# Splitting the third head group four and four, not six and two, between the two column halves of the tensor array

## The chip, the cores and the metric

One core of a Trainium2 chip runs the whole program. The metric is the time of one execution in microseconds (us); the time of a kernel is the median of its runs. "The profiled execution" is one run that was recorded by the hardware profiler: it has a time of its own, and a span, which reaches from its first to its last instruction.

Engines are named as the profile names them: PE is the tensor engine's matmul side, PEld its weight loads, DVE the vector engine, ACT the scalar engine, POOL the GpSimd engine, SP the engine whose queue issues the DMA transfers.

## The reference

Three stages follow each other: a recurrence over 768 steps for 32 heads (4 batches of 8) with a 40x40 state each, an attention layer with routed experts, and a token and channel mixer. The change is in the recurrence alone:

```python
for t in range(S):
    y[:, :, t] = np.einsum('bhd,bhde->bhe', rt, state)
    Sa = np.einsum('bhde,bhe->bhd', state, at)
    state_decay = state * wt[:, :, None, :] - np.einsum('bhd,bhe->bhde', Sa, bt)
    state = state_decay + np.einsum('bhd,bhe->bhde', vt, kt)
```

What comes after it is `_moe_ref` on y and `_moe2_ref` on that. The change touches neither.

## The kernel before

**Chunks and pairs.** The 768 steps are cut into 12 chunks of 64 steps; two chunks (an even and an odd one) make a pair. Inside a chunk, the sequential dependence is a triangular system for each head, whose inverse is worked out on DVE once for a whole pair: `solve` starts with a transpose `tp` (L226), runs 31 steps of two DVE instructions (`pr`, L235, and `x`, L237), and ends with the transpose `xt` (L240). The solve of the next pair runs on DVE, step by step among other work, while the chunks of this pair run on PE. `xt` is needed by the first `xz` of the next even chunk.

**Heads and groups.** The heads are packed three to a group of 120 partitions, so there are 11 groups; the last one holds two heads. `QUADS` collects them into three head groups q = 0, 1, 2 with 4, 4 and 3 groups, that is 12, 12 and 8 heads. This document is about q = 2: groups 8, 9 and 10, heads 24 to 31.

**Sides.** Many matmuls of the recurrence have a stationary operand of only 64 columns (one chunk of 64 steps) or 32 (half a chunk). The array has 128 columns, so such a matmul uses one half of them: side 0 writes PSUM partitions 0 to 63, side 1 partitions 64 to 127. `sides(q, n)` yields who goes to which side: the first two groups of a head group to side 0, the rest to side 1, in turns as long as both have some. With q = 0 and 1 that is six heads and six. With q = 2 it is heads 24 to 29 on side 0 and heads 30 and 31 on side 1, in the order 24, 30, 25, 31, 26, 27, 28, 29. `spans(q)` says which columns of the result lie on which side, for the instructions that read them back: 240 and 240, for q = 2 240 and 80.

**Steps of a chunk that use sides**, for each q:

- `z1` (L276): the state `ST` through the matrix `a`, one matmul for each group, 120 columns (80 for the last), into a PSUM tile `zu`; and in it
- `tv` half 0 (L289): one matmul for each head, 64 columns of weights and 40 moving, added to `zu`; then ACT takes the first 32 rows to `zt` (L293), one instruction for each side;
- `xz` half 0 (L302): one matmul for each head with 32 columns of weights; ACT takes the result to `vu` (L306);
- `tv` half 1 and `xz` half 1: the same for the second 32 rows, again with weights of 32 columns;
- `hh` (L357) and `yy` (L400), for the chunk before: like `z1` and `tv` half 0, into a PSUM tile `y`; DVE multiplies it into `ptt` (L404), one instruction for each side.

Every such fp32 matmul shows up in the trace as two loads and two matmuls.

**What sets the order.** `EVEN` and `ODD` are strings that list the steps of a chunk in the order in which the code issues them (a letter for the step, a digit for q); `x3` to `x5` are `xz` half 1. The order that then stands on each engine is not this one: a scheduler behind the language moves instructions by its own cost estimates, so any edit may move work far from it. Each engine works through its own list in that order. SP's list holds all loads and stores.

Of the kernel before, what the change touches and what calls it, by code (L numbers as in the profile page):

```python
# [28 lines left out]
G = 11  # L29
# [6 lines left out]
ODD = "A z0 x0 v0 v1 z1 z2 r0 h0 x2 t0 m1 x1 m2 s0 v2 r1 y0 h1 m0 r2 M y1 p0 L p1 p2 h2 y2 x3 t1 t2 d0 s2 k0 x5 s1 k1 x4 d2 k2 d1"  # L36
QUADS = [(0, 4), (4, 8), (8, 11)]

def sides(q, n):

    g0, g1 = QUADS[q]
    a, b, e = n * g0, n * (g0 + 2), min(n * g1, 32 if n > 1 else G)
    for i in range(b - a):
        yield a + i, 0, i
        if b + i < e:
            yield b + i, 1, i

def spans(q):

    g0, g1 = QUADS[q]  # L50
    return (0, 120 * g0, 240), (64, 120 * g0 + 240, min(120 * g1, 1280) - 120 * g0 - 240)

def nheads(g):
    return 2 if g == G - 1 else 3
# [15 lines left out]
class Rec:  # L70
# [199 lines left out]
    def z1(s, c, q):  # L270
        nc, t = s.nc, s.T[c // 2]
        zu = s.pz.tile([128, 480], F32, name="zu")
        s.T["zu", q] = zu
        for g, b, i in sides(q, 1):
            k = 40 * nheads(g)
            nc.tensor.matmul(zu[64 * b:64 * b + 64, 120 * i:120 * i + k], t["a"][:k, g, c % 2, :],  # L276
                             s.ST[:k, g, :k], start=(i == 0), stop=False, skip_group_check=True)
        s.tv(c, q, 0)

    def tv(s, c, q, half):  # L280

        nc = s.nc
        zu, sc, vu = s.T["zu", q], s.T["sc", c], s.T["vu", c]
        u = 64 * (1 - c % 2)
        r = slice(u, u + 64) if half else slice(0, 128)
        m = 32 if half else 64
        for h, b, i in sides(q, 3):
            o = 64 * b + 32 * half
            nc.tensor.matmul(zu[o:o + m, 40 * i:40 * i + 40], sc[r, h, 32 * half:32 * half + m],  # L289
                             vu[r, 40 * h:40 * h + 40], start=False, stop=True, skip_group_check=True)  # L290
        d = u + 32 * half
        for b, o, n in spans(q):
            nc.scalar.activation(s.zt[half][d:d + 32, o:o + n], zu[b + 32 * half:b + 32 * half + 32, :n], AF.Copy,  # L293
                                 scale=-1.0)

    def xz(s, c, q, half):
        nc = s.nc
        zu, xt, vu = s.T["zu", q], s.T["xt", c // 2], s.T["vu", c]
        r = slice(64 * (1 - c % 2), 64 * (1 - c % 2) + 64)
        for h, b, i in sides(q, 3):  # L300
            o = 64 * b + 32 * half
            nc.tensor.matmul(zu[o:o + 32, 240 + 40 * i:280 + 40 * i], xt[r, h, :],  # L302
                             s.zt[half][r, 40 * h:40 * h + 40], start=True, stop=True, skip_group_check=True)
        d = 64 * (1 - c % 2) + 32 * half
        for b, o, n in spans(q):
            nc.scalar.activation(vu[d:d + 32, o:o + n], zu[b + 32 * half:b + 32 * half + 32, 240:240 + n], AF.Copy)  # L306
# [44 lines left out]
    def hh(s, c, q):  # L351
        nc = s.nc
        y = s.ps.tile([128, 240], F32, name="y", bufs=1)
        s.T["y", q] = y
        for g, b, i in sides(q, 1):
            k = 40 * nheads(g)
            nc.tensor.matmul(y[64 * b:64 * b + 64, 120 * i:120 * i + k], s.T["r", c][:k, g], s.S[:k, g, :k],  # L357
                             start=(i == 0), stop=False, skip_group_check=True)

    def vut(s, c, q):  # L360
        nc, vu = s.nc, s.T["vu", c]
# [32 lines left out]
    def yy(s, c, q):  # L394
        nc = s.nc
        g0 = QUADS[q][0]
        d = 64 * (c % 2)
        y, sr, kbt = s.T["y", q], s.T["sr", q], s.T["kbt", c]
        for h, b, i in sides(q, 3):
            nc.tensor.matmul(y[64 * b:64 * b + 64, 40 * i:40 * i + 40], sr[:, h - 3 * g0, :], kbt[:, 40 * h:40 * h + 40],  # L400
                             start=False, stop=True, skip_group_check=True)
        xo = s.T["ptt", c // 2]
        for b, o, n in spans(q):
            nc.vector.tensor_tensor(xo[d:d + 64, o:o + n], y[b:b + 64, :n], xo[d:d + 64, o:o + n], OP.mult)  # L404
        if (c % 2, q) == (1, 2):
            nc.sync.dma_start(s.xd[64 * (c - 1):64 * (c + 1)], xo)
# [610 lines left out]
def channel(ctx, tc, ident, psum, ud, c1, c2, out, nb=4):  # L1017
# [19 lines left out]
    def first(s, m):  # L1037
        uh, ul, ur = X[s]
        ms = slice(128 * m, 128 * m + 128)
        p = psum()  # L1040
        mm = [(c1h[:, 0, ms], uh[:, 0]), (c1l[:, 0, ms], uh[:, 0]), (c1h[:, 1, ms], uh[:, 1]),
              (c1l[:, 1, ms], uh[:, 1]), (c1h[:, 2, ms], ur), (c1l[:, 2, ms], ur),
              (c1h[:, 0, ms], ul[:, 0]), (c1h[:, 1, ms], ul[:, 1])]
        for n, (l, r) in enumerate(mm):
            nc.tensor.matmul(p, l, r, start=(n == 0), stop=(n == 7))  # L1045
        hh = wk.tile([128, 512], F32R, name="hh", bufs=LAG + 2)
        hl = wk.tile([128, 512], F32R, name="hl", bufs=LAG + 2)
        nc.scalar.activation(hh, p, AF.Relu)  # L1048
        nc.vector.scalar_tensor_tensor(hl, p, 0.0, hh, op0=OP.max, op1=OP.subtract)  # L1049
        H[s, m] = hh, hl  # L1050
# [101 lines left out]
```

## Time and profile before

| | |
|---|---|
| time, median of 3 runs | 1045.84 us (1043.87 to 1049.55) |
| the profiled execution: its time | 1045.46 us |
| the profiled execution: its span | 1043.7 us |
| mean granted clock of TensorE over the span | 0.969 of full speed |
| busy: PE, PEld, DVE, ACT, POOL | 959.1, 823.1, 674.4, 479.3, 167.7 us |
| matmuls of L289 and L302 in the whole run | 1536 each |
| the chain that ended last: PE, DVE, DMA, ACT | 66%, 19%, 6%, 4% |

The recurrence fills the first 446 us or so, then come the other two stages. A busy share is an average over stages with different limits, and a busy PE is not a PE at its peak: its matmuls are pipelined and overlap. A row that merges several instructions (x24) gives the start of the first and the time until the end of the last. "Granted clock" is the share of TensorE's full clock of 2.4 GHz that the chip granted in a stretch.

### The profile page before, as it was taken

What the parts mean: (1) busy time and instruction counts of PE and PEld (TensorE: products, weight loads), DVE (VectorE), ACT (ScalarE), POOL (GpSimd) and SP (SyncE); (2) the same over time, 40 slices, a digit from 0 to 9 for tenths busy, and PEclk for the clock granted to TensorE, in tenths of its full rate; (3) what the DMA queues carried; (4) which work ended last, traced back from release to release, by engine and by line L of the source; (5) the groups of instructions that cost most, each with busy time, mean ns of one, the idle gap of its engine ahead of it and who ended that gap; (6) DMA issues with size and microseconds to landing.
All of it is one profiled execution on the core that took longest, in us unless ns stands there. A gap on an engine that the chain in (4) does not pass through costs nothing.

```text
span 1043.7 us, 23515 instructions
## 1 busy us (share of the span) xinstructions
PE 959.1 (92%) x9313; PEld 823.1 (79%) x9313; DVE 674.4 (65%) x1793; ACT 479.3 (46%) x1250; POOL 167.7 (16%) x214
## 2 busy tenths in 40 slices
PE   2977997999999999966999999999998999999998
PEld 1646876888888898855877888888787898898987
DVE  6598898887989685747898777566287222222222
ACT  1324544656665665534677667666543121121211
POOL 5000000010000000352234132223255000000000
PEclk9977996999999999979999999999999999999999
DMA  8604422417253323455543441420262101101000
GB/s 172 138 1 96 100 67 74 111 41 170 53 123 74 86 61 117 157 165 145 154 116 99 118 115 31 96 65 26 87 205 63 56 1 56 39 18 57 1 26 26
DMA packets 101031, 88.84 MB, mean 85 GB/s; under 512 B 60785, under 2 KB 91073, under 8 KB 100321
## 3 DMA queue, kind: packets, MB, share of 16 engines
q1 hardware_dynamic: 100921, 87.34, 32.2%
q8 instruction: 74, 1.21, 0.5%
q14 instruction: 36, 0.29, 0.1%
HBM read 54.94 MB, written 15.73 MB: 68 GB/s over the span
## 4 chain that ended last, share of the span: by engine, by line
PE 66%; DVE 19%; DMA 6%; ACT 4%; issue 3%; POOL 1%; SPq 1%; DVEq 0%; ACTq 0%; POOLq 0%
PE pq L1045 12%; PE p L1059 11%; PE psc L205 4%; PE zu L289 3%; PE psc L387 3%; DVE pq L164 3%; PE po L872 3%; PE pq L846 3%; PE zu L302 2%; PE pq L998 2%; PE pm L325 2%; PE zu L276 2%; DVE x L237 2%; PE y L400 2%; DVE pr L235 2%
## 5 line engine op out<-in xcount | busy, mean ns | idle before, releaser
L1049 DVE SCALAR_TENSOR_TENSOR hl<-pq,hh 128x512 fp32r<-128x512 f32 x72 | 49.7, 690 | 153.6 <-ACT hh L1048 153.6
L1048 ACT ACTIVATE hh<-pq 128x512 fp32r<-128x512 f32 x72 | 42.9, 596 | 186.7 <-PE pq L1045 186.7
L1059 PE MATMUL p<-c2h,hh 128*128 128x320 f32 x288 | 90.8, 315 | 0.0
L819 ACT ACTIVATE a<-s,nm 128x512 f32<-128x512 f32 (+3 forms) x128 | 68.7, 542 | 46.4 <-DVE nm L816 21.6
L1059 PE MATMUL p<-c2l,hh 128*128 128x320 f32 x288 | 89.4, 311 | 0.2 <-POOL c2l L635 0.2
L1059 PE MATMUL p<-c2h,hl 128*128 128x320 f32 x288 | 89.5, 311 | 0.1
L306 ACT ACTIVATE vu<-zu 32x240 f32<-32x240 f32 (+1 forms) x144 | 48.8, 339 | 55.2 <-PE zu L302 45.1
L293 ACT ACTIVATE zt<-zu 32x240 f32<-32x240 f32 (+1 forms) x144 | 48.7, 338 | 51.7 <-PE zu L289 49.6
L814 DVE TENSOR_REDUCE nm<-s 128x1 f32<-128x512 f32 (+3 forms) x128 | 62.0, 500 | 15.7 <-PE s L813 10.8
L164 DVE TENSOR_TENSOR pq<-w,pq 120x88 f32<-120x88 f32 x186 | 61.2, 329 | 9.7 <-DMA w<-in_w 5.8
L832 POOL TENSOR_TENSOR a<-a,rs 128x128 f32<-128x128 f32 (+1 forms) x64 | 45.6, 734 | 126.6 <-DVE rs L827 84.5
L235 DVE TENSOR_TENSOR pr<-tp,x 128x31 f32<-128x31 f32 (+15 forms) x186 | 63.0, 339 | 3.8 <-DVE tp L226 0.5
L237 DVE TENSOR_TENSOR x<-x,pr 128x31 f32<-128x31 f32 (+15 forms) x186 | 63.2, 340 | 3.3
L289 PE MATMUL zu<-vu,sc 64*32 64x40 f32 (+1 forms) x1536 | 61.3, 220 | 1.2 <-ACT vu L306 1.2
L302 PE MATMUL zu<-zt,xt 64*32 64x40 f32 x1536 | 48.3, 211 | 12.5 <-DVE pq L161 6.8
L1045 PE MATMUL pq<-uh,c1h 128*128 128x512 f32 x144 | 57.6, 400 | 0.8 <-DVE ul L666 0.8
L289 PEld LDWEIGHTS zu<-vu,sc 64*32 64x32 f32 (+1 forms) x1536 | 53.2, 127 | 6.2 <-ACT vu L306 2.9
L1059 PEld LDWEIGHTS p<-c2h,hh 128*128 128x128 f32 x288 | 54.5, 189 | 3.7 <-DVE o L1062 1.2
L1045 PE MATMUL pq<-uh,c1l 128*128 128x512 f32 x144 | 57.1, 396 | 0.0
L1059 PEld LDWEIGHTS p<-c2l,hh 128*128 128x128 f32 x288 | 54.5, 189 | 2.9 <-POOL c2l L635 0.5
L387 PE MATMUL psc<-rbd,vut 120*128 120x192 f32 (+1 forms) x264 | 54.6, 341 | 1.9 <-DVE sr L391 1.6
L302 PEld LDWEIGHTS zu<-zt,xt 64*32 64x32 f32 x1536 | 40.3, 117 | 20.1 <-issue 12.8
(206 smaller groups left out, 2504.4 us busy)
## 6 DMA issues: line engine op xcount, KB each, us to landing
kb<-in_kb SPq DMA_DIRECT2D x5, 1320.0 KB
kh<-hb SPq DMA_DIRECT2D x64, 96.0 KB
cv<-in_c SPq DMA_DIRECT2D x18, 256.0 KB
w<-in_w SPq DMA_DIRECT2D x6, 660.0 KB
a<-in_a SPq DMA_DIRECT2D x6, 660.0 KB
r<-in_r SPq DMA_DIRECT2D x12, 330.0 KB
rbd<-in_r SPq DMA_DIRECT2D x36, 110.0 KB
vu<-in_v SPq DMA_DIRECT2D x12, 320.0 KB
```

What stands on the lines that cost most here:

```text
L164: e.tensor_tensor(two(pq, i + 1, x + 29 - 2 * i), two(t["w"], i, 31 - 2 * i), two(pq, i, x + 31 - 2 * i), OP.mult)
L235: v.tensor_tensor(prv, tp[:, j + 1:, j:j + 1].to_broadcast([128, n, j + 1]), x[:, j:j + 1, :j + 1].to_broadcast([128, n, j + 1]), OP.mult)
L237: v.tensor_tensor(x[:, j + 1:, :j + 1], x[:, j + 1:, :j + 1], prv, OP.subtract)
L289: nc.tensor.matmul(zu[o:o + m, 40 * i:40 * i + 40], sc[r, h, 32 * half:32 * half + m], vu[r, 40 * h:40 * h + 40], start=False, stop=True, ...
L302: nc.tensor.matmul(zu[o:o + 32, 240 + 40 * i:280 + 40 * i], xt[r, h, :], s.zt[half][r, 40 * h:40 * h + 40], start=True, stop=True, skip_gr ...
L306: nc.scalar.activation(vu[d:d + 32, o:o + n], zu[b + 32 * half:b + 32 * half + 32, 240:240 + n], AF.Copy)
L387: nc.tensor.matmul(ps[:, n:n + nheads(g), :], vt[:k, g - g0, :], rbd[:k, g, :nheads(g), :], start=True, stop=True)
L814: nc.vector.tensor_reduce(nm[:, x:x + 1], s, axis=AX.X, op=OP.max, negate=True)
L819: nc.scalar.activation(a[:, n0:n1], s, AF.Exp, bias=nm[:, -1:] if nb_ == 2 else nm[:, :1], accum_out=sm[:, x, i % 2:i % 2 + 1])
L1045: nc.tensor.matmul(p, l, r, start=(n == 0), stop=(n == 7))
L1049: nc.vector.scalar_tensor_tensor(hl, p, 0.0, hh, op0=OP.max, op1=OP.subtract)
L1059: nc.tensor.matmul(Y[s][i], hs[x][:, ts], w[:, k], start=(k + n == 0), stop=(k == 11 and n == 2))
```

## The change

`sides` now counts heads, half to each side: for q = 2 heads 24 to 27 on side 0 and 28 to 31 on side 1, in turns. The border then runs through group 9, so `z1` and `hh`, which work by groups, need a new helper `blocks` that cuts a group where a side ends: group 8 (120 columns) and the first 40 columns of group 9 on side 0, the other 80 columns of group 9 and group 10 (80 columns) on side 1: four matmuls where three were. `spans` gives 160 and 160 columns for q = 2. For q = 0 and 1 the three functions yield what they did. Lines after them stand 13 lower.

```diff
-def sides(q, n):
+def blocks(q):
 
     g0, g1 = QUADS[q]
-    a, b, e = n * g0, n * (g0 + 2), min(n * g1, 32 if n > 1 else G)
-    for i in range(b - a):
-        yield a + i, 0, i
-        if b + i < e:
-            yield b + i, 1, i
+    m, e = 3 * g0 + (12 if g1 < G else 8) // 2, min(3 * g1, 32)
+    out = [[], []]
+    for z, (l, h) in enumerate(((3 * g0, m), (m, e))):
+        x = l
+        while x < h:
+            y = min(h, 3 * (x // 3) + 3)
+            out[z].append((x // 3, 40 * (x % 3), 40 * (x % 3 + y - x), z, 40 * (x - l)))
+            x = y
+    return [x for p in zip(*out) for x in p]
+
+def sides(q):
+
+    g0, g1 = QUADS[q]
+    n = (min(3 * g1, 32) - 3 * g0) // 2
+    for i in range(n):
+        yield 3 * g0 + i, 0, i
+        yield 3 * g0 + n + i, 1, i
 
 def spans(q):
 
     g0, g1 = QUADS[q]
-    return (0, 120 * g0, 240), (64, 120 * g0 + 240, min(120 * g1, 1280) - 120 * g0 - 240)
+    n = (min(120 * g1, 1280) - 120 * g0) // 2
+    return (0, 120 * g0, n), (64, 120 * g0 + n, n)
...
-        for g, b, i in sides(q, 1):
+        for g, l, h, b, o in blocks(q):
             k = 40 * nheads(g)
-            nc.tensor.matmul(zu[64 * b:64 * b + 64, 120 * i:120 * i + k], t["a"][:k, g, c % 2, :],
-                             s.ST[:k, g, :k], start=(i == 0), stop=False, skip_group_check=True)
+            nc.tensor.matmul(zu[64 * b:64 * b + 64, o:o + h - l], t["a"][:k, g, c % 2, :],
+                             s.ST[:k, g, l:h], start=(o == 0), stop=False, skip_group_check=True)
...
-        for h, b, i in sides(q, 3):
+        for h, b, i in sides(q):
...
-        for g, b, i in sides(q, 1):
+        for g, l, h, b, o in blocks(q):
             k = 40 * nheads(g)
-            nc.tensor.matmul(y[64 * b:64 * b + 64, 120 * i:120 * i + k], s.T["r", c][:k, g], s.S[:k, g, :k],
-                             start=(i == 0), stop=False, skip_group_check=True)
+            nc.tensor.matmul(y[64 * b:64 * b + 64, o:o + h - l], s.T["r", c][:k, g], s.S[:k, g, l:h],
+                             start=(o == 0), stop=False, skip_group_check=True)
```

On PE, in the fourth chunk, this is `z1` and `tv` half 0 for q = 1 and 2 before; the last three rows but one are `z1` of q = 2, the last is its `tv`, eight matmuls:

```order
L276 MATMUL zu<-ST,a 64x120 x4
L289 MATMUL zu<-vu,sc 64x40 x12
L276 MATMUL zu<-ST,a 64x120
L276 MATMUL zu<-ST,a 64x80
L276 MATMUL zu<-ST,a 64x120
L289 MATMUL zu<-vu,sc 64x40 x8
```

The same place now:

```order
L289 MATMUL zu<-ST,a 64x120 x4
L302 MATMUL zu<-vu,sc 64x40 x12
L289 MATMUL zu<-ST,a 64x120
L289 MATMUL zu<-ST,a 64x80
L289 MATMUL zu<-ST,a 64x40
L289 MATMUL zu<-ST,a 64x80
L302 MATMUL zu<-vu,sc 64x40 x8
```

`z1` of q = 2 has a matmul more and narrower ones; `tv` keeps its eight, whose sides an order does not show.

The scheduler also moved whole instructions. On DVE, around the `xt` of the fifth solve, which the ninth chunk waits for, before (`ptt` is `yy`'s result of the chunk before, `sc` and `sr` are masked products that DVE takes out of PSUM):

```order
L235 TENSOR_TENSOR pr<-tp,x 128x31
L237 TENSOR_TENSOR x<-x,pr 128x31
L240 STREAM_TRANSPOSE xt<-x 128x32x32
L404 TENSOR_TENSOR ptt<-y,ptt 64x240 x2
L210 TENSOR_TENSOR sc<-psc,mask 128x128
L391 TENSOR_TENSOR sr<-psc,mask 128x384 x3
L391 TENSOR_TENSOR sr<-psc,mask 128x128
L404 TENSOR_TENSOR ptt<-y,ptt 64x240 x2
```

The same place now:

```order
L404 TENSOR_TENSOR sr<-psc,mask 128x384
L248 TENSOR_TENSOR pr<-tp,x 128x60
L250 TENSOR_TENSOR x<-x,pr 128x2x30
L404 TENSOR_TENSOR sr<-psc,mask 128x384
L248 TENSOR_TENSOR pr<-tp,x 128x31
L404 TENSOR_TENSOR sr<-psc,mask 128x384
L250 TENSOR_TENSOR x<-x,pr 128x31
L404 TENSOR_TENSOR sr<-psc,mask 128x128
L253 STREAM_TRANSPOSE xt<-x 128x32x32
L417 TENSOR_TENSOR ptt<-y,ptt 64x240 x2
```

The four `sr` (and, a few rows further up, one `sc` and two `ptt`) that followed `xt` now stand ahead of it. At most other places the order on DVE is the old one or differs by neighbours that changed places.

## Rows read from the trace of the kernel before

**Rows 1.** The page: the chain that ended last, by engine.

```profile
PE 66%; DVE 19%; DMA 6%; ACT 4%; issue 3%; POOL 1%; SPq 1%; DVEq 0%; ACTq 0%; POOLq 0%
```

**Rows 2.** Windows: stretch, length, busy PE PEld DVE ACT POOL, granted clock, DMA share, GB/s.

```profile
71.70:100.00 28.30, 22.18 (x309) 19.63 (x310) 25.39 (x64) 15.21 (x42) 1.50 (x4) 0.66 0.32 73
100.00:147.00 47.00, 45.95 (x639) 39.56 (x638) 42.02 (x109) 24.82 (x61) 2.70 (x4) 1.00 0.36 86
147.00:166.20 19.20, 10.72 (x91) 8.02 (x91) 18.84 (x61) 5.38 (x8) 0.41 (x3) 0.82 0.31 85
166.20:191.40 25.20, 24.16 (x439) 21.83 (x440) 17.56 (x40) 17.55 (x51) 2.25 (x3) 0.80 0.45 106
191.40:216.70 25.30, 24.77 (x361) 21.86 (x360) 24.54 (x69) 13.65 (x38) 1.16 (x1) 1.00 0.27 66
216.70:254.00 37.30, 35.42 (x601) 31.18 (x601) 29.89 (x74) 24.23 (x61) 2.66 (x5) 0.96 0.52 122
254.00:284.20 30.20, 29.72 (x435) 26.25 (x434) 29.10 (x82) 16.30 (x42) 1.16 (x1) 0.99 0.29 66
284.20:303.30 19.10, 18.17 (x338) 15.81 (x338) 17.17 (x43) 12.40 (x32) 1.50 (x4) 1.00 0.28 72
303.30:342.80 39.50, 37.77 (x612) 34.05 (x610) 35.74 (x88) 23.27 (x67) 2.32 (x2) 1.00 0.44 99
342.80:362.00 19.20, 18.75 (x338) 16.12 (x339) 9.82 (x20) 13.39 (x31) 1.12 (x2) 1.00 0.37 99
362.00:398.00 36.00, 35.33 (x602) 31.45 (x600) 31.31 (x87) 22.52 (x66) 1.16 (x1) 1.00 0.19 51
398.00:432.00 34.00, 33.38 (x695) 29.28 (x696) 20.05 (x41) 20.75 (x55) 8.30 (x6) 1.00 0.47 145
...
162.00:172.00 10.00, 6.19 (x170) 5.78 (x167) 9.58 (x24) 5.82 (x14) 1.50 (x4) 0.50 0.43 135
```

**Rows 3.** Timeline of PEld alone, fourth chunk: start, time to the last end, count.

```profile
184.09 0.83 PEld L289 LDWEIGHTS zu<-vu,sc 128*64 128x64 f32 x24
184.83 0.40 PEld L276 LDWEIGHTS zu<-ST,a 120*64 120x64 f32 x6
185.10 0.93 PEld L289 LDWEIGHTS zu<-vu,sc 128*64 128x64 f32 x16
195.46 0.50 PEld L302 LDWEIGHTS zu<-zt,xt 64*32 64x32 f32 x24
197.26 0.40 PEld L357 LDWEIGHTS y<-S,r 120*64 120x64 f32 x8
```

**Rows 4.** Groups by line and form, first 620 us: count, busy us, mean ns.

```profile
L306 ACT ACTIVATE vu<-zu 32x240 f32<-32x240 f32 x120 | 43.3, 360 | 54.9 <-PE zu L302 45.1 <-issue 8.3
L302 PEld LDWEIGHTS zu<-zt,xt 64*32 64x32 f32 x1536 | 40.3, 117 | 20.1 <-issue 12.8 <-DVE xt L240 4.2 <-ACT zt L293 0.9
L289 PEld LDWEIGHTS zu<-vu,sc 128*64 128x64 f32 x768 | 33.3, 138 | 2.9 <-issue 2.2
L306 ACT ACTIVATE vu<-zu 32x80 f32<-32x80 f32 x24 | 5.5, 229 | 0.3
```

**Rows 5.** Timeline of PE alone, at two stops: the bracket is the idle time before.

```profile
166.17 1.80 PE L302 MATMUL zu<-zt,xt 64*32 64x40 f32 x40 [3.81 <-DVE xt L240]
...
251.73 0.58 PE L367 MATMUL pm<-ident,vu 128*120 128x128 f32 x2 [1.53 <-issue]
```

**Rows 6.** Timeline of DVE alone, around the fifth `xt`.

```profile
340.80 1.96 DVE L240 STREAM_TRANSPOSE xt<-x 128x1024 f32<-128x1024 f32 x1
342.79 0.83 DVE L404 TENSOR_TENSOR ptt<-y,ptt 64x240 f32<-64x240 f32 x2
343.64 0.29 DVE L210 TENSOR_TENSOR sc<-psc,mask 128x128 f32<-128x128 f32 x1
343.85 0.55 DVE L391 TENSOR_TENSOR sr<-psc,mask 128x384 f32<-128x384 f32 x1
347.35 0.56 DVE L391 TENSOR_TENSOR sr<-psc,mask 128x384 f32<-128x384 f32 x1 [2.95 <-PE psc L387]
```

More of the change, by code (lines that the diff above doesn't have):

```diff
@@ L299, in xz @@
         r = slice(64 * (1 - c % 2), 64 * (1 - c % 2) + 64)
-        for h, b, i in sides(q, 3):
+        for h, b, i in sides(q):
             o = 64 * b + 32 * half
@@ L398, in yy @@
         y, sr, kbt = s.T["y", q], s.T["sr", q], s.T["kbt", c]
-        for h, b, i in sides(q, 3):
+        for h, b, i in sides(q):
             nc.tensor.matmul(y[64 * b:64 * b + 64, 40 * i:40 * i + 40], sr[:, h - 3 * g0, :], kbt[:, 40 * h:40 * h + 40],
```

## The prediction

> **What bounds the kernel now.** I read the page first: PE carries 66% of the chain that ended last, DVE 19% [rows 1]. That is an average over three stages, and the recurrence has both engines busy, so it does not say who sets the time there. The windows do [rows 2]. I cut the recurrence at the moments when an even chunk gets its solve (166.2, 216.7, 284.2, 342.8 and 398 us) and between, and look at what DVE has left in each.
>
> Four windows leave DVE much idle time: 166.2 to 191.4 (7.6 us), 216.7 to 254 (7.4), 342.8 to 362 (9.4) and 398 to 432 (13.9), while PE is busy for 95 to 98%. There PE sets the pace: 115.7 us. Four leave DVE almost none: 147 to 166.2 (0.4 us), 191.4 to 216.7 (0.8), 254 to 284.2 (1.1) and 71.7 to 100 (2.9 of 28.3, with PE busy for only 78%). There the solve and the decay on DVE set it: 103 us. The other four, 141.6 us, are mixed: DVE is idle for 15.4 us of them.
>
> **What the change does to one batch.** The timeline of weight loads shows it best [rows 3]. The `tv` of q = 1 (24 loads, 12 on each side) takes 0.83 us from the first load to the end of the last. The `tv` of q = 2 right behind it has only 16 loads, but takes 0.93 us, no less. So a batch does not cost its number of loads, but that of its fuller side: six heads, 12 loads, in both. The two sides run beside each other.
>
> From this, one load's step on a side: the last load itself takes 0.138 us [rows 4], so 12 loads in 0.83 us are 11 steps of (0.83 - 0.138)/11 = 0.063 us. With four heads on each side the fuller side has 8 loads, not 12: 4 x 0.063 = 0.25 us less for a `tv` half 0 of q = 2, and for a `yy`, whose operands have the same sizes. For loads of 32 columns, 24 of them take 0.50 us and one 0.117 [rows 3, 4]: a step of (0.50 - 0.117)/11 = 0.035 us, and 4 x 0.035 = 0.14 us less for an `xz` half 0, a `tv` half 1 and an `xz` half 1.
>
> `z1` and `hh`: eight loads or six both take 0.40 us [rows 3], since both have four on the fuller side; a step is (0.40 - 0.138)/3 = 0.087 us, longer than above because 120 columns move, not 40. Side 0 now has two with 120 columns and two with 40, which I take at 0.063: 2 x 0.024 = 0.05 us less. The bounds are nothing (if the 40-column ones cost as much) and 0.17 (if they cost nothing). Side 1 gets four with 80 columns. The trace has no 80-column step apart, so I put it halfway, 0.075: with its `tv`, side 1 then takes 4 x 0.075 + 8 x 0.063 = 0.80 us, and side 0 2 x 0.087 + 10 x 0.063 = 0.80. The added matmul costs nothing as long as the sides run beside each other; if they did not, its two loads would be 0.126 us.
>
> Each of the 12 chunks has a `tv` half 0 and a `yy` (0.50), three batches of 32-column loads (0.42) and a `z1` and a `hh` (0.10): 1.02 us, in all 12.2 us of tensor time at full clock.
>
> **What it does to the other engines.** ACT reads a side's 240 columns in 360 ns and 80 in 229 [rows 4], 589 together. A 160-column read lies halfway on this line, 295, and two make 590: nothing gained or lost. The same for DVE's `ptt`. ACT starts a little earlier because the last matmul of a batch ends earlier; that is the saving already counted.
>
> **What it does to the order.** The scheduler moved work. On most engines neighbours changed places, which I price at nothing: PE stays full across them. One move I price: the fifth `xt` now stands behind two `ptt`, one `sc` and four `sr` that followed it: 0.83 + 0.29 + 3 x 0.55 + 0.29 = 3.1 us of DVE work (the last `sr` is as large as the `sc`) [rows 6]. That is the cost from above, if PE then waits. From below it is nothing: right after that work DVE stood idle for 2.95 us, waiting for PE [rows 6], so PE was the later one, and it has the products that fed these seven left to do before `xt` as well. I take nothing, and keep 3.1 us either way for the range.
>
> **How much of 12.2 us arrives.** The batches are spread evenly, 12.2 us over the 374 us from 71.7 to the recurrence's end at about 446: 0.033 us saved per us. Where PE sets the pace, all of it arrives: 115.7 x 0.033 = 3.8 us, and 0.2 more because the clock was 0.80 in the first of these windows, where each step takes longer. Where DVE sets it, nothing: the PE then only waits more. Of the mixed windows' 4.6 us I take half, 2.3, since the chain changes hands there; none and all are the bounds. The last 14 us, `yy` of the last chunk, give 0.5. The sum is 6.8 us. The two later stages get the same work in nearly the same order and move up as they are. Against the profiled execution's own 1045.46 us that is 1038.7; its time is 0.4 us under the median of the runs shown, which I neglect.
>
> **The rivals.**
>
> *DVE takes it all.* PE's savings only lengthen its waits for DVE until the last solve is done, and only what lies behind 398 us arrives: 48 x 0.033 = 1.6 us, 1043.9 us. For it: DVE busy for 89% and more in seven of twelve windows [rows 2]. Against it: 38 us of DVE idle time in four windows before and after those, in which it waits for PE.
>
> *All of it arrives.* 1045.5 - 12.2 = 1033.3 us. For it: the chain runs on PE for two thirds. Against it: the 103 us in which DVE has no idle time to give.
>
> *Slower: PE gets ahead of the solve and loses its clock.* In the windows that DVE sets, PE ends earlier and then stands still before the next `xt`. Such a stop was 3.81 us long at 166.17 [rows 5], and the granted clock was 0.50, the lower level of 1.2 GHz, from 162 to 172 us, and 0.80 in the mean of the window behind the stop [rows 2]: 25.2 x 0.20 = 5.0 us of clock lost. A stop of 1.53 us at 251.73 [rows 5] lies in a window with 0.96. So it decides somewhere between stops of 1.5 and 3.8 us, and the savings of one DVE-bound window are 103/4 x 0.033 = 0.8 us, under that; the later fifth `xt` could add its 3.1. Two such places would give 1045.5 - 4.0 + 10.0 = 1051.5 us (4.0 being what the PE-bound windows give).
>
> *The sides do not run beside each other.* If weight loads of the two column halves queued behind each other, a batch would cost its number of loads, which stays at 16, and the added matmul of `z1` and `hh` would cost 24 x 0.126 = 3.0 us: 1048.5 us. Rows 3 speak against it: 16 loads took no less than 24. The Trainium skill (TensorE: Matmul & The Clock Gate, Part 3: Packing small matmuls, The mechanism) has this rule: a weight load overlaps a running matmul only if the two lie in different row groups, and both sides here use the same rows. The trace does not agree with it for column halves.
>
> **How the numbers follow.** Chances: the forecast 0.58, DVE takes it all 0.20, all arrives 0.12, slower by the clock 0.07, sides in line 0.03. The forecast's own range is the mixed windows' none and all (4.5 to 9.1 us saved) and the 3.1 us of the moved `xt` either way: 1033.3 to 1044.1. Over 0.5% (5.2 us, about what a measurement of this kernel can tell from no change) means under 1040.6 or over 1051.0. Three quarters of the forecast lie under 1040.6: 0.43, and with all of it arriving 0.12 the chance of faster is 0.55. The last quarter, DVE taking it all and the sides in line make 0.38 for no change; slower has 0.07. The range from 1032.5 to 1046 holds the first three cases and leaves out the last two, with their 0.10, and the edges.
>
> **What would show it.** In the trace of the changed kernel: the 16 loads of a `tv` half 0 or a `yy` of q = 2 in about 0.68 us (8 a side, and the 0.1 us that its first loads start early, as 0.93 against 0.83 now), not 0.93; busy time of PE in the recurrence down by some 10 us; the even chunks' `xt` earlier by growing amounts, 1 us at 216.7 and 4 to 5 at 398; the recurrence's end near 439. The prediction is wrong if the `xt` come at the old times while PE's stops before them grow, or if a window of the recurrence has a clock under 0.9 that had 1.00, or if the moved `xt` comes 3 us later while PE is idle.

## The result, and the profile after

The changed kernel takes 1052.7 us (median of 16 runs), the kernel before beside it 1044.55 (16 runs). Runs more than 1.5% above the fastest of their kernel, here one of 1188.85 us at a clock of 0.738, stand in the medians but not in the ratios and ranges, here and below. The other 15 took 1042.89 to 1057.88 us. The ratio is 1.0055, 95% interval 1.0033 to 1.0078: half a per cent slower, where I had forecast 1038.7 us. The profiled execution took 1057.88 us, its span is 1056.2.

Lines behind the edit have other numbers now: `z1` is L289, `tv` L302, `xz` L315, `hh` L370, `yy` L413. The timeline of weight loads at the place of [rows 3] (start, time to the last end, count):

```profile
184.85 0.40 PEld L289 LDWEIGHTS zu<-ST,a 120*64 120x64 f32 x8 [0.17 <-issue]
185.21 0.83 PEld L302 LDWEIGHTS zu<-vu,sc 128*64 128x64 f32 x24
185.96 0.40 PEld L289 LDWEIGHTS zu<-ST,a 120*64 120x64 f32 x8
186.23 0.59 PEld L302 LDWEIGHTS zu<-vu,sc 128*64 128x64 f32 x16
```

The 16 loads of the third group's `tv` take 0.59 us, not 0.93, while the 24 of the second still take 0.83. The added load pair of `z1` shows in the count, x8 where x6 stood, and not in the time. ACT's and DVE's reads of the third group are now two of 160 columns (count, busy us, mean ns):

```profile
L319 ACT ACTIVATE vu<-zu 32x160 f32<-32x160 f32 x48 | 14.1, 294 | 37.7 <-PE zu L315 31.7 <-issue 5.5
L417 DVE TENSOR_TENSOR ptt<-y,ptt 64x160 f32<-64x160 f32 x24 | 7.7, 321 | 6.1 <-PE y L413 5.7
```

So the tensor work became shorter, as worked out. The windows of the recurrence (the view of [rows 2]: stretch, length, busy PE PEld DVE ACT POOL, granted clock, DMA share, GB/s) show what went wrong:

```profile
216.00:252.00 36.00, 33.25 (x587) 28.62 (x586) 28.82 (x71) 22.50 (x58) 0.44 (x3) 0.97 0.53 124
252.00:286.00 34.00, 33.37 (x442) 29.41 (x441) 27.57 (x79) 15.74 (x44) 2.32 (x2) 0.88 0.24 57
286.00:307.00 21.00, 20.15 (x283) 16.72 (x284) 12.48 (x33) 9.49 (x24) 1.12 (x2) 0.67 0.15 39
307.00:354.00 47.00, 44.99 (x699) 39.39 (x699) 42.21 (x106) 30.18 (x79) 2.70 (x4) 1.00 0.46 103
354.00:373.00 19.00, 18.02 (x286) 15.14 (x287) 6.93 (x14) 8.88 (x24) 1.12 (x2) 0.73 0.27 71
373.00:411.00 38.00, 37.74 (x654) 32.81 (x652) 33.04 (x90) 25.17 (x71) 1.16 (x1) 1.00 0.22 57
411.00:432.00 21.00, 20.27 (x366) 16.97 (x364) 10.12 (x21) 11.08 (x30) 2.87 (x2) 0.84 0.59 178
...
292.00:302.00 10.00, 10.00 (x107) 7.87 (x107) 3.89 (x11) 2.76 (x8) 0.00 (x0) 0.50 0.11 24
...
71.70:461.00 389.30, 360.08 (x5616) 311.70 (x5613) 310.10 (x786) 215.92 (x564) 32.57 (x39) 0.89 0.37 92
```

Behind the solves of chunks 6, 8 and 10 (windows that begin at 286, 354 and 411) the granted clock is 0.67, 0.73 and 0.84. The windows of before that answer to them, from 284.2, 342.8 and 398, all had 1.00 [rows 2]. The window from 252 has 0.88, where before had 0.99 from 254. From 292 to 302 us it is 0.50, the lower level of 1.2 GHz, while PE is busy for 10.00 of 10 us: by its busy time PE looks perfect there. The last row is the whole recurrence; the same view of before, where it ended about 14 us sooner, is

```profile
71.70:447.00 375.30, 348.84 (x5578) 304.66 (x5578) 310.54 (x787) 213.71 (x560) 32.32 (x39) 0.95 0.37 93
```

Length times clock is 375.3 x 0.95 = 356.5 us before and 389.3 x 0.89 = 346.5 after. At full clock the recurrence has become 10 us shorter (give or take 4, as the clocks have two digits; windows of 1 us, added up, make it 9); it lasts 14 us longer because the clock took some 43 us of it, not some 19.

PE's timeline, the view of [rows 5], shows the shorter batches and the stops (the bracket is the idle time before):

```profile
186.30 0.64 PE L302 MATMUL zu<-vu,sc 128*64 128x40 f32 x16
...
201.01 0.64 PE L413 MATMUL y<-kbt,sr 128*64 128x40 f32 x16
...
226.61 0.48 PE L315 MATMUL zu<-zt,xt 64*32 64x40 f32 x16
...
250.16 0.74 PE L315 MATMUL zu<-zt,xt 64*32 64x40 f32 x15 [2.75 <-issue]
...
288.71 0.91 PE L315 MATMUL zu<-zt,xt 64*32 64x40 f32 x40 [0.55 <-DVE pq L177]
289.93 0.37 PE L302 MATMUL zu<-vu,sc 64*32 64x40 f32 x10 [0.31 <-ACT vu L319]
...
356.13 0.42 PE L355 MATMUL pm<-ident,ST 120*120 120x120 f32 x2 [0.66 <-ACT S L361]
356.48 0.91 PE L315 MATMUL zu<-zt,xt 64*32 64x40 f32 x40
357.70 0.37 PE L302 MATMUL zu<-vu,sc 64*32 64x40 f32 x10 [0.32 <-ACT vu L319]
```

The stops around the three solves are not long. A stop of 0.55 us, 40 small matmuls in 0.91, a stop of 0.31, more small ones: after that the clock is at its lower level. (The stop of 2.75 us ahead of 250.16 is another one, behind no solve; the kernel before has one of 1.53 us at a like place [rows 5], and the 0.88 above lies behind it.) The runs say the same. Of the 15 the slowest, 1056.4 to 1057.9 us, have a mean clock of 0.946 to 0.948, the fastest, 1042.9 to 1043.9, one of 0.959 to 0.961: 15 us over 0.015 of clock. The profiled execution of before had 0.969.

### The profile page after: what moved, and what is told of

Read it like the earlier page. It is cut to its first block, busy times and chain, and to the rows that moved or that the text cites. A ratio compares the mean times of both kernels' runs of the same rounds, so it can differ in the third digit from the quotient of the medians.

```text
span 1056.2 us, 23622 instructions
## 1 busy us (share of the span) xinstructions
PE 970.5 (92%) x9361; PEld 829.4 (79%) x9361; DVE 673.2 (64%) x1793; ACT 480.6 (46%) x1250; POOL 168.4 (16%) x214
## 4 chain that ended last, share of the span: by engine, by line
PE 40%; DVE 4%; DMA 3%; ACT 1%; issue 1%; SPq 1%; POOL 0%; DVEq 0%; ACTq 0%; POOLq 0%
PE pq L1058 11%; PE p L1072 11%; PE po L885 3%; PE pq L859 2%; PE pq L787 2%; PE pq L1011 2%; PE pq L1024 2%; PE pq L900 2%; PE pq L740 1%; PE s L823 1%; PE pq L676 1%; PE s L824 1%; DMA wf<-w 1%; DVE nm L827 1%; DMA kh<-hb 1%
## 5 line engine op out<-in xcount | busy, mean ns | idle before, releaser
L319 ACT ACTIVATE vu<-zu 32x160 f32<-32x160 f32 (+1 forms) x144 | 48.8, 339 | 59.5 <-PE zu L315 51.5
L218 PE MATMUL psc<-abd,kb 120*128 120x192 f32 (+1 forms) x242 | 59.9, 387 | 2.7 <-DVE sc L223 2.7
L315 PE MATMUL zu<-zt,xt 64*32 64x40 f32 x1536 | 48.5, 217 | 14.7 <-DVE pq L174 6.9
L315 PEld LDWEIGHTS zu<-zt,xt 64*32 64x32 f32 x1536 | 39.3, 123 | 24.6 <-issue 14.7
L302 PE MATMUL zu<-vu,sc 64*32 64x40 f32 (+1 forms) x1536 | 56.9, 222 | 1.2 <-ACT vu L319 1.2
L223 DVE TENSOR_TENSOR sc<-psc,mask 128x384 f32<-128x384 f32 x72 | 36.2, 513 | 33.7 <-PE psc L218 32.5
```

Of the source, the lines that this page charges most:

```text
L218: nc.tensor.matmul(ps[:, n:n + nheads(g), :], t["kb"][:k, g, c % 2, :], abd[:k, g, :nheads(g), :], start=True, stop=True)
```

## The experiments

The change has two halves: the split, and the order that the scheduler made of it. To part them, a kernel is built twice: once to read the order of each engine, once with the split wanted, each instruction bound behind the one that precedes it in that order (issue order only, no wait). Every ratio is to the kernel before, run beside it.

```diff
+    _, order = build(False)
+    nc, _ = build(True, order)
...
+                tc.add_manual_dep(at[l], last.name, mybir.DependencyInfo(
+                    mybir.DependencyClass.NoSync, mybir.DependencyReason.DATA), reason="order")
```

**New split, old order**, and its reverse, **old split, new order** (`build(True)` first, then `build(False, order)`):

> This kernel has the four-and-four split, but every engine and every queue issues in the order of the kernel before (the added matmul of z1 and hh stands right behind its neighbour). Theory, the order: the changed kernel's granted clock fell to 0.50 to 0.75 in windows behind the even chunks' solves at 292, 362 and 412 us because the scheduler's new order put the small 64x40 matmuls there side by side, without the large ones that stood between them before. Then this kernel keeps a clock of 1.00 in these windows, its mean clock is 0.969 or more as before, its recurrence ends near 439 us instead of 446 and 461, and its time is 1036 to 1041 us, my old forecast. Rival, the split itself: shorter batches let PE run ahead, stand still and lose the clock whatever the order. Then the low windows come back behind the even chunks, the mean clock is about 0.95, and the time is 1048 to 1056.

> The reverse: the six-and-two split of the kernel before, issued in the order of the changed kernel. Theory, the order: the clock falls behind the even chunks' solves as in the changed kernel, its mean clock is 0.95, and since the batches of the third group are long again the time is that of the changed kernel and some 7 more, 1055 to 1063 us. Rival, the split itself: clock and time are those of the kernel before, 0.965 to 0.97 and 1042 to 1047 us.

The first took 1046.03 us, ratio 1.0009 (0.9982 to 1.0036). Its 12 runs fall into two groups: three of 1037.6 to 1039.4 us with a clock of 0.965 to 0.967, which is the old forecast, and nine of 1040.9 to 1048.1 with 0.955 to 0.961. The profiled execution, 1046.16 us, is one of the nine:

```profile
281.00:301.00 20.00, 18.72 (x352) 16.34 (x353) 18.38 (x49) 13.86 (x36) 1.51 (x4) 1.00 0.32 77
338.00:358.00 20.00, 19.11 (x351) 16.13 (x349) 11.25 (x24) 13.94 (x32) 1.12 (x2) 1.00 0.42 106
358.00:392.00 34.00, 33.05 (x600) 29.42 (x598) 30.07 (x83) 22.10 (x65) 1.16 (x1) 1.00 0.20 48
392.00:410.00 18.00, 17.34 (x282) 14.97 (x283) 8.65 (x20) 7.84 (x23) 2.53 (x2) 0.62 0.25 69
```

Behind chunks 6 and 8 the clock stays, as the theory wanted; behind chunk 10 it falls, as the rival wanted. The reverse took 1061.59 us, ratio 1.0164 (1.0124 to 1.0204), inside the 1055 to 1063 expected, with a clock of 0.945 to 0.961:

```profile
280.00:300.00 20.00, 19.13 (x275) 16.03 (x275) 10.96 (x32) 8.12 (x23) 1.12 (x2) 0.66 0.15 43
348.00:370.00 22.00, 21.03 (x265) 17.83 (x264) 6.16 (x13) 10.07 (x25) 1.12 (x2) 0.61 0.31 86
370.00:408.00 38.00, 37.92 (x637) 33.39 (x635) 32.37 (x89) 24.19 (x70) 1.16 (x1) 1.00 0.18 43
408.00:426.00 18.00, 17.26 (x292) 14.71 (x293) 8.61 (x18) 8.67 (x24) 2.87 (x2) 0.72 0.43 118
```

In the executions profiled the new order loses the clock behind all three solves, whatever the split; the split alone loses it only behind the last, and by the mean clocks not in every run. In the new order the split is worth 1.0164 against 1.0055, 1.1%. Binding the instructions to an order costs little by itself: a kernel further down, with the split and the order of before and eight matmuls added, has 1.0024.

**PE kept fuller around the solve.** Added matmuls that nobody needs, ahead of the first `xz` of a chunk, in the stop where PE waits for the solve; `FILL` says how many in which chunk:

```diff
+        if (q, half) == (2, 0):
+            sc = s.T["sc", c].rearrange("p s t -> p (s t)")
+            for _ in range(FILL.get(c, 0)):
+                m = nc.tensor.matmul(zu[:, 240:480], s.ident, sc[:, :240], start=True, stop=True, skip_group_check=True)
...
```

> The changed kernel in its own order, with two matmuls of 128x240 added ahead of the first xz of chunks 4, 6, 8 and 10, in the place where PE stands still for the solve (0.55 to 0.66 us at 288 and 356 us). They write columns that the xz behind them overwrite, so the outputs stay as they are. By the spin's row (22 records of 128x512 in 9.61 us, two to a matmul) one takes 0.41 us, two 0.82, so 0.2 to 0.3 us a chunk stick out, 1 us in all. Theory, the clock: what costs the changed kernel its time is the lower clock behind those solves, and a fuller PE there keeps it up. Then the granted clock is 1.00 in the windows behind 288, 356 and 412 us, the mean clock goes from 0.948 to 0.965 or more, and the time from 1052.7 to 1036 to 1042. Rival, the order itself (stalls by neighbours that changed places) or the fifth xt: clock or not, the time stays over 1047.

> The four-and-four split in the order of the kernel before, with the same eight matmuls added. Without them its runs fell into two groups: 1037.6 to 1040.9 us at a mean clock of mostly 0.965 to 0.967, and 1044.6 to 1048.1 at 0.955 to 0.961 (8 of 12). Theory, the clock: with them the clock stays in all runs, mean 0.965 or more, and the time is 1037 to 1041 in nearly all of them, a ratio to before of 0.995 to 0.998. Rival: the two groups have another cause; they stay, with a median over 1044.

> Control: the kernel before, six-and-two split and own order, with the same eight matmuls added. It lost no clock behind the solves of chunks 6, 8 and 10, so by the theory there is nothing to give back: 1 us for the matmuls that stick out, against up to 1.7 us for the 3.4 us at half clock around 252 us if that goes too: 1042 to 1046, clock 0.966 to 0.972. If it also falls by 5 us or more, then the added matmuls help by something else than what the change broke.

One thing in these expectations is not so. `start=True` begins an accumulation in the whole bank of `zu`, so the second `tv` half of the third group, behind it, replaces sums instead of adding to them: in the chunks with added matmuls a part of that group's product is left out. (The Trainium skill, PSUM — Partial Sum Buffer, The four PSUM rules, has the rule: a first matmul clears the written-marks of the bank over the partition quadrants that it writes; no trace here shows these marks.) The instructions and their order are the same with and without it, so the times are read as they are; the last four kernels have `start=False` and leave nothing out.

The changed kernel with eight added matmuls took 1046.38 us, 1.0012 (0.9981 to 1.0043), at 0.959 to 0.964. Against its 1.0055 without them that is 0.4% less, for work that does nothing. The clock came back behind chunks 6 and 8, but not behind chunk 10:

```profile
287.00:307.00 20.00, 19.63 (x363) 16.47 (x362) 16.93 (x45) 13.96 (x36) 1.51 (x4) 1.00 0.31 77
307.00:350.00 43.00, 40.58 (x640) 35.52 (x638) 38.49 (x95) 24.25 (x65) 3.23 (x3) 1.00 0.43 97
350.00:369.00 19.00, 18.52 (x352) 15.65 (x353) 10.34 (x25) 14.67 (x38) 0.21 (x2) 1.00 0.31 90
369.00:402.00 33.00, 32.88 (x584) 28.95 (x582) 28.58 (x77) 18.86 (x55) 1.16 (x1) 1.00 0.21 52
402.00:422.00 20.00, 19.39 (x353) 16.39 (x353) 8.20 (x18) 11.56 (x31) 2.88 (x2) 0.83 0.62 196
```

The time lies above the 1036 to 1042 expected: one solve was not held, and the eight are not free. In the control, the kernel before with them, they cost 0.24% (1046.62 us, 1.0024, 1.0005 to 1.0044), 2.5 us where I had 1. New split and old order with them took 1042.46 us, 0.9983 (0.9957 to 1.0009), at 0.962 to 0.969: the group at 0.955 to 0.961 is gone, but the time lies over the 1041 expected, by less than the eight cost the control. Between these two kernels only the split differs: 0.9983 against 1.0024, 0.4% or 4.2 us.

**The reverse: PE made emptier around the solve,** in the kernel before:

```diff
+        if LATE and p > 2:
+            m = v.tensor_tensor(tp[:, :24], tp[:, :24], tp[:, :24], OP.mult)
...
         xt = wk.tile([128, 32, 32], F32, name="xt")
```

> The kernel before, split and order unchanged, with one added DVE product right ahead of the xt of chunks 6, 8 and 10 (tp times tp, 128x768, into the tp that nobody reads any more; the outputs stay as they are). By the rows of the solve's own products (0.37 us for 207 columns, 0.18 for 31) it takes 0.94 us, so PE's stops ahead of the xz, 0.43 to 0.63 us in the kernel before, become 1.4 to 1.6. Theory, the clock hangs on how sparse PE is around the solve: with stops of that size the granted clock falls behind some of these solves, as it did in the changed kernel, and the time is 1049 to 1062 us, more than the 2.8 us of the three products. Rival: stops of 1.5 us cost only themselves; the clock stays at 0.965 and the time is 1044 to 1048.

It took 1057.99 us in the median of six runs, ratio 1.0106 (1.0054 to 1.0158); the five in the ratio have 1048.5 to 1062.3 us at a clock of 0.963 down to 0.949. In the profiled one, the fastest, the stops became 0.74, 1.16 and 0.78 us, not the 1.4 to 1.6 expected. Chunk 8 lost the clock, behind the stop of 1.16 us that had 0.43 before (first row below); chunks 6 and 10 kept it.

```profile
342.90 1.02 PE L302 MATMUL zu<-zt,xt 64*32 64x40 f32 x40 [0.43 <-DVE xt L240]
...
338.80 1.02 PE L324 MATMUL zu<-zt,xt 64*32 64x40 f32 x40 [1.16 <-DVE xt L260]
340.12 0.51 PE L311 MATMUL zu<-vu,sc 64*32 64x40 f32 x13 [0.31 <-ACT vu L328]
```

```profile
280.00:300.00 20.00, 19.16 (x348) 16.72 (x349) 17.95 (x46) 13.30 (x35) 1.44 (x4) 1.00 0.31 74
338.00:358.00 20.00, 18.89 (x235) 15.77 (x236) 5.88 (x13) 8.04 (x19) 1.12 (x2) 0.58 0.13 30
```

So three products of 0.95 us each on another engine cost 1.1%, 11 us and not 2.8. The clock of PE goes with it: from the fastest of the five runs to the slowest it is 14 us for 0.014 of mean clock.

**A version that beats both.** New split, old order, matmuls added only where clock is lost: two for chunk 10; then eight and five more in the long stops ahead of chunks 0 and 2; then the same without the accumulation begun; then one more for chunks 4, 6 and 8 each; and the kernel before with the same 15.

> A version that might beat both: four-and-four split, order of the kernel before, and two added matmuls of 128x240 ahead of the first xz of chunk 10 alone, where 8 of 12 runs of the same kernel without them lost their clock. Theory: the clock stays, 0.965 or more, and the time is 1037.5 to 1040.5, a ratio to before of 0.993 to 0.997. Rival: the runs lose it elsewhere, and the time is 1043 to 1047.

> The same with eight more of these matmuls in the stop of 6.7 us ahead of chunk 0's first xz and five in the stop of 3.8 us ahead of chunk 2's, where PE only waits for DVE and the clock is at its lower level in every run (63 to 84 us and 156 to 173 us). At half clock one takes 0.82 us, so they take 6.6 and 4.1 us at most and 0.3 us stick out. Theory: the clock comes back one or two of its steps earlier behind chunk 2's solve and the mean clock rises to 0.970 or more; 2 to 4 us less than with chunk 10's two alone, 1034 to 1038. Rival: the clock comes back no earlier, and the time is the same within 1 us or 1 to 3 us longer.

> The version of the run before it with 15 added matmuls (eight ahead of chunk 0's first xz, five ahead of chunk 2's, two ahead of chunk 10's; four-and-four split, order of the kernel before). The one difference: the added matmuls no longer begin an accumulation of their own in the bank of zu. Where they did, the second tv half of the third group behind them replaced the sums in that bank instead of adding to them, so a part of the third group's product was left out in the chunks that have them; now nothing is left out. Work and order are the same, so by either theory the time is: 1033 to 1037 us, a ratio to before of 0.989 to 0.995, clock 0.970 to 0.975.

> The same with one more such matmul ahead of the first xz of chunks 4, 6 and 8. In its profiled execution the version with 15 of them lost the clock for 13.7 us behind chunk 6's solve (280 us). Theory, the clock: these three cost under 0.3 us each (two cost the kernel before 0.6 a chunk) and keep it there, so the median falls by up to 2 us, to 1032 to 1036, and the slowest runs, near 1041, are gone. Rival: one of them is too little, and the time is 1 us longer, 1035 to 1038.

> Control: the kernel before, six-and-two split, with the same 15 added matmuls. It tells what of the gain is the clock at chunks 0 and 2 and what is the split. If the split is worth at a held clock what its batches save (4 us by the two filled kernels, 6.8 by the old forecast), this one has a ratio of 0.994 to 0.998, 1037 to 1041 us, 4 to 7 us more than with the four-and-four split. Rival: the split is worth nothing, the clock is all; then it has 1033 to 1037 us like the other.

| kernel | median us | ratio to before | 95% interval | mean clock of the runs |
|---|---|---|---|---|
| two added | 1039.95 | 0.9957 | 0.9932 to 0.9982 | 0.958 to 0.967 |
| 15 added | 1035.13 | 0.9921 | 0.9892 to 0.9951 | 0.966 to 0.978 |
| 15 added, nothing left out | 1033.46 | 0.9892 | 0.9844 to 0.9941 | 0.970 to 0.976 |
| 18 added | 1036.83 | 0.9921 | 0.9889 to 0.9954 | 0.968 to 0.975 |
| kernel before, 15 added | 1042.21 | 0.9961 | 0.9932 to 0.9990 | 0.970 to 0.976 |

Two matmuls turn 1.0009 into 0.9957, 15 into 0.9892, the fastest version of this study. With two the time is the one expected, though the clock was not held at 0.965 in all runs. One more for three chunks brings no gain that shows: 1036.83 us lies in the rival's range, and the interval of its ratio holds 0.9892 too. With 15 and nothing left out, chunk 10's window, 0.62 above, is

```profile
390.00:408.00 18.00, 17.41 (x364) 14.48 (x362) 9.34 (x21) 10.39 (x28) 2.53 (x2) 1.00 0.50 140
```

The last row of the table is the cleanest measure of the split: same order, same added work, same clock, and 0.9961 against 0.9892. That is 0.7% or 7.2 us, against the forecast's 6.8. (With 18, three more than the control has, it is 0.9921, 0.4% or 4.2 us.) The intervals of the two ratios just overlap, but the runs themselves, taken beside each other, do not: 1032.94 to 1038.49 us with the split, 1040.68 to 1045.32 without. The control's time lies 1 us above the 1037 to 1041 expected. The other 0.4%, from the matmuls in the control alone, the kernel before could have had as well; in its profiled execution the clock is at 1.00 from 166 to 191 us, where it had 0.80 [rows 2].

**The new order, clock held.** The changed kernel in its own order with 23 added matmuls:

> The changed kernel in its own order with 23 added matmuls: eight, five, two, two, two and four ahead of the first xz of chunks 0, 2, 4, 6, 8 and 10, none of which begins an accumulation, so that nothing is left out. It asks what the new order costs where the clock is held: the same split in the old order, held, has a ratio to before of 0.989 to 0.992. Theory, the order costs some time of its own (3 to 4 us by the two filled kernels of the first set, whose clocks were 0.962 and 0.965): 1036 to 1041 us, a ratio of 0.993 to 0.998, at a clock of 0.968 or more. Rival, the order costs only by the clock: then it has the old order's 1033 to 1037 us. If the clock stays under 0.965 here, this run does not tell them apart.

1040.51 us, 0.9970 (0.9940 to 1.0000), at 0.960 to 0.969. Its four fastest runs, at 0.966 to 0.969, took 1036.6 to 1038.8; the three at 0.960 to 0.962 took 1045.2 to 1048.1. The clock was not held in all runs (in the profiled one, 1045.97 us, it fell behind chunks 6 and 10, each time for some 10 us), so whether the new order costs anything but clock stays open. The four fastest leave it little: they lie among the old order's runs with 18 added, 1032.0 to 1040.2.

## Why the prediction was wrong

**The batches: right, and in size.** On PE's timeline, above, a `tv` half 0 of 16 now takes 0.64 us, as does a `yy`, and an `xz` half 1 takes 0.48. The same view of before has

```profile
136.43 0.92 PE L289 MATMUL zu<-vu,sc 128*64 128x40 f32 x16
...
153.82 0.89 PE L400 MATMUL y<-kbt,sr 128*64 128x40 f32 x16
...
227.46 0.61 PE L302 MATMUL zu<-zt,xt 64*32 64x40 f32 x16
```

That is 0.28, 0.25 and 0.13 us saved, where the prediction had 0.25, 0.25 and 0.14. By the weight loads of the `tv` it is more, 0.59 us where I expected 0.68. The fuller side sets a batch: 24 loads, 12 a side, take 0.83 us, 16 loads took 0.93 with 12 on one side and take 0.59 with 8 on each. The rival "the sides do not run beside each other" is out, and the Trainium skill's rule that it rested on (TensorE: Matmul & The Clock Gate, Part 3: Packing small matmuls, The mechanism) does not hold here for the two column halves.

**The other engines: right.** ACT's 160-column read takes 294 ns (295 expected), and DVE's two take 321 each, 642 together, where 240 and 80 columns took 403 and 243.

**The share that arrives: about right, once the clock is equal.** 7.2 us at a held clock in the 15-matmul pair, 4.2 in the pair with eight (each known to 3 to 6 us only, by the intervals), for 6.8 with bounds of 4.5 and 9.1. "DVE takes it all" (1.6 us) and "all arrives" (12.2) are further from the 7.2; the 4.2 is as near to 1.6 as to 6.8. PE's busy time did not fall by 10 us as I had said it would show; it rose, 348.84 to 360.08 us in the rows above, since records at half clock are longer (a `yy` of 16 takes 1.08 us at 292.30, 0.64 at 201.01). Length times clock shows the 10 us.

**The moved fifth `xt`: inside its bound, as far as it shows.** With the clock held behind chunks 6 and 8, DVE's timeline has the fourth and fifth `xt` at 285.32 and 347.03 in the new order and at 283.37 and 340.92 in the old, the same split in both: 61.7 us from one to the next against 57.6, so 4.2 us later. The sixth comes 52.3 us after the fifth, against 54.1. If that is the same work coming back, some 2.4 us stay, inside the 3.1 either way. PE did not stand idle for it: it was busy for 59.59 us from 285.3 to 347.03 in the new order, and for 54.70 from 283.4 to 340.9 in the old.

**The step that failed** is "On most engines neighbours changed places, which I price at nothing: PE stays full across them." PE did stay full by its busy time, and the moves still cost the clock: the new order under the old split is 1.6% slower, 17 us, and needless matmuls added to the changed kernel give 0.4% back with eight and 0.85% with 23. The split has its part in it too: in the old order it loses the clock behind chunk 10, and 1.0009 is left where 0.993 was forecast. What I had named as the mark of a wrong forecast, a window under 0.9 that had 1.00, is there three times. Beside it fell the rival's condition, "it decides somewhere between stops of 1.5 and 3.8 us", by which I gave a loss of clock 0.07. I had taken the length of a stop for what counts and read it from two stops, both wrongly, as the trace of before shows (windows as in [rows 2], then PE's timeline as in [rows 5]):

```profile
152.00:162.00 10.00, 6.45 (x48) 4.86 (x48) 9.81 (x35) 1.06 (x3) 0.00 (x0) 0.86 0.24 55
...
242.00:252.00 10.00, 8.47 (x173) 7.27 (x172) 8.31 (x20) 7.66 (x22) 0.00 (x0) 0.97 0.94 215
252.00:262.00 10.00, 10.00 (x159) 9.08 (x158) 7.90 (x15) 3.78 (x10) 1.16 (x1) 0.86 0.38 92
...
398.07 1.02 PE L302 MATMUL zu<-zt,xt 64*32 64x40 f32 x40 [0.63 <-DVE xt L240]
399.40 0.51 PE L289 MATMUL zu<-vu,sc 64*32 64x40 f32 x13 [0.31 <-ACT vu L306]
```

The stop of 3.81 us began at 162.36, and the clock had fallen before it. Around the stop of 1.53 us it fell as well; the mean of a window of 37 us hid that. And stops of 0.63 and 0.31 us in chunk 10 kept 1.00 [rows 2], while in the rows of the changed kernel the clock falls behind stops of 0.55 and 0.31 us with 40 matmuls of 64x40 between them and more behind. The length of the stop does not tell the two apart. The Trainium skill (TensorE: Matmul & The Clock Gate, Part 1: The HAM clock gate, A second HAM failure mode) tells of a kernel whose PE idles for moments between groups of matmuls often enough to swing between the two levels; the trace here agrees, with those stops and a clock of 0.50.

My rival also looked in the wrong place, the windows that DVE sets. The clock fell in the windows that follow a solve; I had put two of the three down as set by PE and one as mixed. There a us of half clock costs about half a us: 0.015 of mean clock, 16 us of a 1050 us run, went with 15 us of time.

**What stays open.** Why the same kind of stop keeps the clock in one order and loses it in another is not settled. The stop and the small matmuls ahead of chunk 6 read nearly alike in the two orders, and one and the same program (new split, old order) has runs of either kind by their mean clock, three of 12 at 0.965 to 0.967. Of the kernel before's 104 runs beside the experiments, 17 had a clock under 0.962, so it seems to stand near the same edge. That the split brings chunk 10 over it in most runs is shown, as far as mean clocks tell, by the pair with the same order; by which part of it was not tried. Nor was it tried which engine's new order does it.

## What to carry to other kernels

A saving on the tensor engine is worth what the clock behind it leaves: read the granted clock window by window before and after, and multiply it into the lengths, before any busy share is believed. Where a solve or another wait is followed by a run of small matmuls the clock may be near falling even if PE reads as busy for 95 to 100%; there a small edit or a reordering can cost more than it saves, and a few needless matmuls in the wait are a cheap test of it, and here a cure. When a scheduler answers an edit with a new order, build the edit in the old order too: the two effects had opposite signs here. The split gained 4 to 7 us at a held clock and the order lost 17 under the old split; they do not add up, since in the new order the split was worth 1.1%, and about half a per cent was lost in the end.

## What the runs showed of the hardware that was not expected

The granted clock was 0.50 for ten us in which PE's records show no idle time at all (292 to 302 us). Two needless matmuls of 128x240 in 1046 us made a kernel 0.5% faster (1.0009 to 0.9957). Three DVE products of 0.95 us each made one 1.1% slower.
